# A stored list of 133 numbers that shifts the planned order of issue is replaced by a list of 201 others (clustered attention and a two-layer network, one core)

## The chip, the cores and the metric

The kernel runs on one core of one Trainium2 chip. The metric is device time in microseconds (us), from the first to the last instruction of one execution with what lies around it. Three runs of the kernel before are shown.

## The reference, cut to what matters

```python
# q, k, v: (4, 8, 768, 64) f32; centroids: (8, 16, 64); w_in (512, 2048); w_out (2048, 512)
q_assign = argmax(q_n . c_n)          # cluster of each query, k_assign the same for keys
mask   = q_assign[:, :, :, None] == k_assign[:, :, None, :]
scores = where(mask, q k^T / 8, -1e9)
attn   = softmax(scores)              # over 768 keys
x      = (attn v) as (3072, 512)      # heads side by side
h      = x @ w_in
g      = where(h >= 1, h, where(h <= -1, 0, (h + 1)^2 / 4))
out    = g @ w_out                    # (3072, 512) f32
```

All is float32 outside; inside, most products are made from pairs of float16 tiles (a high and a low half).

## The kernel before, in words

**Tiles.** The tokens are cut into 12 units `u` (4 batches of 3 chunks, 256 queries each). For each unit there are 4 pairs of heads. For one pair of heads the kernel makes 4 score tiles of 128 queries by 768 keys (`at_scores`, line 915): four products of 384 columns on TensorE into the PSUM tile `pair`, then one pass of VectorE that writes the tile to `sS` with its row minimum `sbi`. `at_soft` (line 946) exponentiates on ScalarE, makes the high half on ScalarE and the low half on GpSimd (`hl`), and sends `hl` through a transposing DMA to `pT`. For unit 0 (`whole`) the transposes are TensorE products instead. `at_av` (line 994) multiplies `pT` with the values into `banka`: 8 small and 36 larger products. Then follows the network: for each of 8 slabs `f`, `ffn1` (line 1149) does 24 products of 256 columns, VectorE and ScalarE apply the function, GpSimd makes the low half of `g`, and `ffn2` (line 1189) does 12 products of 512 columns.

**Preparation.** Before they are used, keys, queries and values are scaled and split (`k_split`, `q_split`, `v_split`), clusters assigned (`k_assign`, `q_assign`, `q_pairs`), and the 16 slabs of weights unpacked by integer passes on VectorE (`w_bits`, line 1081: tiles `w`, `word`, `wk`, `o`) and split on ScalarE and GpSimd (`w_split`, line 1138). The weights are prepared once, in the first fifth of the execution.

**The order of issue.** The functions don't issue anything: a `Recorder` (line 78) keeps each operation, or each group of products, as a node with an engine, a cost and the nodes it depends on. Each call of a function is an event (`ev`); sorted by the step at which it was entered there are 852 of them, and the set-up before them counts as one more, so 853. `issue` (line 328) makes the order: nine rounds of a forward and a backward pass of a list scheduler give each node a due time in ns, each number of the list `NUDGES` (line 45) shifts some due times, and a last forward pass with these due times as priorities fixes the order in which the instructions go to each engine's queue. Then the recorded calls are made in that order, all from line 342, so every row of the profile bears that line. Engines take their queues in order. All DMAs are issued from SP's queue, so their order is fixed by the same pass.

**What one number does** (`nudge`, line 314). It is hashed to a first event `lo`, a count of 1 to 128 events, a stride of 1, 2 or 5 and a size of 500 to 8000 ns; the due times of the nodes in these events move by a hashed share of plus or minus the size:

```python
lo, every, size = b % len(names), (1, 2, 5)[(a >> 8) % 3], float(500 << ((a >> 16) % 5))
...
    if lo <= i < lo + (1 << (a % 8)) and not (i - lo) % every:
        r = c if c >> 8 & 1 else mix(c + i * 7919)
        prio[x] += ((r & 0xFFFF) / 32768.0 - 1.0) * size
```

The forward pass (line 215) lets each engine take, among nodes whose inputs have come, the one with the smallest due time. Its model of the chip (`Machine`, line 345) knows a cost per instruction, a fixed lag per engine, the DMA queue, a slower TensorE after little work, and a turn that VectorE and GpSimd take with some of their passes.

Of the kernel before, what the change touches and what calls it, by code (L numbers as in the profile page):

```python
# [42 lines left out]
LOOK, MARGIN = 0.4, 4000  # L43
BASE = 9
NUDGES = (
# [17 lines left out]
)  # L63
TILED = 248

# [1283 lines left out]
```

## Time and profile before

| | us |
|---|---|
| runs of the kernel before | 855.63, 849.04, 852.69 (median 852.69) |
| span of the profiled execution | 851.1 |
| TensorE (PE) busy in it | 810.1 |
| VectorE (DVE), ScalarE (ACT), GpSimd (POOL) busy | 635.3, 656.1, 536.2 |

The page gives the span of the profiled execution, and no time of its own beside it. PE's busy time counts a product from its start to its modelled end; idle time of PE is the span less this. A releaser is what ended an idle time. Times inside a view are us from the start of the span.

### The profile page before, as it was taken

What the parts mean: (1) busy time and instruction counts of PE and PEld (TensorE: products, weight loads), DVE (VectorE), ACT (ScalarE), POOL (GpSimd) and SP (SyncE); (2) the same over time, 40 slices, a digit from 0 to 9 for tenths busy, and PEclk for the clock granted to TensorE, in tenths of its full rate; (3) what the DMA queues carried; (4) which work ended last, traced back from release to release, by engine and by line L of the source; (5) the groups of instructions that cost most, each with busy time, mean ns of one, the idle gap of its engine ahead of it and who ended that gap; (6) DMA issues with size and microseconds to landing.
All of it is one profiled execution on the core that took longest, in us unless ns stands there. A gap on an engine that the chain in (4) does not pass through costs nothing.

```text
span 851.1 us, 18767 instructions
## 1 busy us (share of the span) xinstructions
PE 810.1 (95%) x7052; PEld 558.9 (66%) x7052; DVE 635.3 (75%) x1400; ACT 656.1 (77%) x1166; POOL 536.2 (63%) x510
## 2 busy tenths in 40 slices
PE   3787998999999999999999999999999999999998
PEld 3455675666775676766776667667766667676664
DVE  6999999879886877678888766678888766544322
ACT  7778989899987788688778788788778688776232
POOL 1112799879986678667666778656677667666122
PEclk9999999999999999999999999999999999999999
DMA  9968898798999879898998988999999887665100
GB/s 311 269 138 246 225 204 213 157 172 194 186 172 159 186 128 205 171 185 169 201 187 165 168 160 177 197 170 199 204 155 161 150 162 126 119 123 111 20 25 25
DMA packets 404763, 142.50 MB, mean 167 GB/s; under 512 B 372800, under 2 KB 396352, under 8 KB 404672
## 3 DMA queue, kind: packets, MB, share of 16 engines
q1 hardware_dynamic: 404672, 141.30, 82.1%
q8 instruction: 55, 0.90, 0.4%
q14 instruction: 36, 0.29, 0.1%
HBM read 40.40 MB, written 6.29 MB: 55 GB/s over the span
## 4 chain that ended last, share of the span: by engine, by line
PE 77%; DVE 12%; DMA 4%; issue 3%; ACT 2%; POOL 1%; SPq 0%; DVEq 0%; POOLq 0%; ACTq 0%
PE pair L342 39%; PE banka L342 10%; PE banki L342 9%; PE bankj L342 9%; PE bankh L342 9%; DVE sS L342 3%; DVE w L342 2%; DMA pT<-hl 1%; DVE bankh L342 1%; DMA q<-qn 1%; DMA kv<-n 1%; ACT sS L342 1%; DVE mx L342 1%; DMA kv<-x 1%; POOL hl L342 1%
## 5 line engine op out<-in xcount | busy, mean ns | idle before, releaser
L342 POOL TENSOR_TENSOR hl<-sS,hl 128x768 f16<-128x768 f32 x176 | 301.2, 1716 | 120.7 <-ACT hl L342 105.5
L342 PE MATMUL pair<-w,g 128*128 128x512 f16 (+1 forms) x1120 | 276.7, 392 | 0.7 <-DVE g L342 0.7
L342 ACT ACTIVATE sS<-sS,sbi 128x768 f32<-128x768 f32 x192 | 179.2, 933 | 73.9 <-DVE sbi L342 70.5
L342 DVE CUSTOM_DVE_ANT_0 sS<-pair,zero,er 128x768 f32<-128x768 f32 x192 | 194.3, 1012 | 53.6 <-PE pair L342 32.9
L342 PEld LDWEIGHTS <-w 128*128 128x128 f16 x2112 | 204.9, 98 | 42.7 <-issue 4.5
L342 PEld LDWEIGHTS <-g 128*128 128x128 f16 x1056 | 101.1, 98 | 107.2 <-issue 2.0
L342 PE MATMUL pair<-kv,q 128*128 128x384 f16 x768 | 158.1, 329 | 11.1 <-ACT pT L342 5.0
L342 ACT CAST hl<-sS 128x768 f16<-128x768 f32 x176 | 144.4, 825 | 9.3 <-DMA pT<-hl 7.9
L342 POOL TENSOR_TENSOR g<-r,g 128x512 f16<-128x512 f32 x80 | 96.4, 1205 | 56.4 <-ACT g L342 50.6
L342 PEld LDWEIGHTS <-q 128*128 128x128 f16 x992 | 78.9, 98 | 66.6 <-issue 22.8
L342 PE MATMUL banka<-pT,kv 128*64 128x256 f16 (+1 forms) x1680 | 105.7, 279 | 0.3 <-DMA pT<-hl 0.3
L342 PEld LDWEIGHTS <-kv 128*64 128x64 f16 (+1 forms) x1824 | 92.3, 108 | 5.0 <-DMA kv<-x 1.7
L342 ACT ACTIVATE r<-r,f_ra,f_rs 128x512 f32<-128x512 f32 x80 | 64.8, 810 | 35.0 <-DVE r L342 34.3
L342 PE MATMUL bankj<-x,w 128*128 128x256 f16 (+1 forms) x424 | 59.1, 292 | 0.6 <-DVE g L342 0.4
L342 ACT CAST g<-r 128x512 f16<-128x512 f32 x80 | 48.8, 611 | 11.8 <-DVE r L342 5.9
L342 POOL TENSOR_TENSOR qn<-qn,phi 128x256 f16<-128x256 f16 x48 | 31.9, 684 | 30.3 <-DVE phi L342 19.9
L342 PE MATMUL bankh<-x,w 128*128 128x256 f16 (+1 forms) x376 | 46.7, 277 | 0.6 <-DVE zs L342 0.5
L342 PE MATMUL banki<-x,w 128*128 128x256 f16 (+1 forms) x288 | 40.3, 291 | 0.9 <-DVE r L342 0.9
L342 PE MATMUL banki<-wk,w 128*128 128x256 f16 x312 | 37.0, 273 | 0.0
L342 ACT ACTIVATION_READ_ACCUMULATOR sS<-sS,sbi 128x1 f32 x192 | 36.1, 188 | 0.0
L342 ACT ACTIVATE q<-q,phi 128x512 f16<-128x512 f16 x48 | 33.0, 711 | 2.8 <-DVE phi L342 0.8
L342 DVE TENSOR_SCALAR r<-banki,f_lo,f_hi 128x512 f32<-128x512 f32 x27 | 21.8, 806 | 16.0 <-PE banki L342 10.0
(262 smaller groups left out, 1099.8 us busy)
## 6 DMA issues: line engine op xcount, KB each, us to landing
w<-in_moe_w_out_dram SPq DMA_DIRECT2D x14, 512.0 KB, 4.8
q<-in_q_dram SPq DMA_DIRECT2D x12, 512.0 KB, 5.4
kv<-in_k_dram SPq DMA_DIRECT2D x16, 384.0 KB, 4.0
kv<-in_v_dram SPq DMA_DIRECT2D x16, 384.0 KB, 4.4
out_dram<-o SPq DMA_DIRECT2D x11, 512.0 KB, 3.6
w<-in_moe_w_in_dram SPq DMA_DIRECT2D x10, 512.0 KB, 6.1
word<-in_moe_w_in_dram SPq DMA_DIRECT2D x6, 512.0 KB, 4.3
o<-in_v_dram SPq DMA_DIRECT2D x8, 384.0 KB, 3.9
```

The costliest lines, as they stand in the source:

```text
L342: fn(*args, **kw)
```

## The change

The 133 numbers of `NUDGES` are replaced by 201 others, none of which was in the old list. The old numbers are close together (2100000010 to 2100031687), in ascending order; the new ones are spread over 32 bits and in no order. They are said to come from a new search with many more evaluated orders, and with replays in which results come late at random. Nothing else is edited: the same nodes, costs, buffers, and the same model.

```diff
 NUDGES = (
-    2100000010, 2100000020, 2100000029, 2100000041, 2100000053, 2100000117, 2100000135, 2100000137,
...
-    2100027979, 2100028867, 2100030528, 2100031297, 2100031687,
+    2274640804, 3868013745, 1465309218, 3554455116, 1849672550, 1493886748, 838542255, 1618903720, 2841474855,
...
+    3685093637, 53219364, 3824218690,
 )
```

Hashing the numbers as `nudge` does tells which events they touch: the old list touches 1,734 events in all (an event counted each time it is touched), 130 of them among the first 213 of the 853; the new one 2,378, and 840 of them among the first 213. Event 213 lies at step 41, in the third unit of the twelve.

## Rows read from the trace of the kernel before

**Rows 1.** The page: the span, and busy time of each engine with its share.

```profile
span 851.1 us, 18767 instructions
PE 810.1 (95%) x7052; PEld 558.9 (66%) x7052; DVE 635.3 (75%) x1400; ACT 656.1 (77%) x1166; POOL 536.2 (63%) x510
```

**Rows 2.** Busy time by stretch, six stretches that make up the span. Columns: stretch, length, then busy us (and instructions) of PE, PE's weight loads, DVE, ACT and POOL, the granted clock of PE as a share of full speed, the DMA engines' busy share, GB/s.

```profile
0.00:22.10 22.10, 8.91 (x123) 8.09 (x124) 13.98 (x46) 16.66 (x27) 3.17 (x28) 1.00 0.93 310
22.10:85.10 63.00, 46.39 (x443) 31.18 (x441) 60.14 (x151) 47.44 (x83) 11.08 (x18) 0.95 0.85 217
85.10:190.00 104.90, 99.22 (x693) 67.84 (x692) 95.17 (x171) 95.28 (x157) 85.82 (x55) 0.98 0.89 194
190.00:340.00 150.00, 149.12 (x1350) 102.50 (x1350) 123.55 (x282) 129.09 (x235) 120.04 (x109) 1.00 0.93 176
340.00:839.30 499.30, 498.73 (x4417) 345.93 (x4414) 339.94 (x750) 364.61 (x663) 313.79 (x300) 1.00 0.79 150
839.30:851.10 11.80, 7.78 (x37) 3.33 (x34) 2.53 (x4) 3.00 (x5) 2.31 (x2) 0.94 0.12 44
```

**Rows 3.** The same columns for the stretch between 20.5 and 163.8 alone.

```profile
20.50:163.80 143.30, 121.91 (x934) 82.91 (x932) 136.19 (x263) 119.67 (x197) 77.86 (x59) 0.96 0.88 211
```

**Rows 4.** What PE waited for between 22.1 and 85.1: us in total, times, longest.

```profile
PE pair L342 <- ACT sS L342: 5.5, 8, 0.9
PE pair L342 <- ACT pT L342: 5.0, 7, 1.4
PE pair L342 <- DMA kv<-n: 1.4, 1, 1.4
```

**Rows 5.** The same between 85.1 and 190, all rows.

```profile
PE pair L342 <- DVE sbi L342: 3.4, 1, 3.4
PE pair L342 <- ACT pT L342: 0.9, 1, 0.9
PE banki L342 <- DVE r L342: 0.9, 1, 0.9
PE pair L342 <- DVE g L342: 0.7, 1, 0.7
PE bankj L342 <- DVE g L342: 0.4, 1, 0.4
```

**Rows 6.** The three stretches in which PE's granted clock fell, with the columns of rows 2.

```profile
37.55:40.96 3.41, 3.41 (x22) 1.79 (x22) 3.10 (x10) 1.48 (x3) 1.30 (x4) 0.55 1.13 352
78.50:81.92 3.42, 3.42 (x25) 2.91 (x24) 3.42 (x6) 2.50 (x6) 0.00 (x0) 0.55 0.91 308
143.36:146.77 3.41, 2.96 (x13) 2.29 (x11) 2.84 (x6) 3.12 (x7) 3.41 (x4) 0.55 1.02 261
```

**Rows 7.** DVE's passes by form between 0 and 85: count, busy us, mean ns of one, and idle time before them.

```profile
L342 DVE CUSTOM_DVE_ANT_0 sS<-pair,zero,er 128x768 f32<-128x768 f32 x18 | 18.2, 1013 | 1.4 <-PE pair L342 1.3
L342 DVE SCALAR_TENSOR_TENSOR w<-w 128x1024 uint32<-128x1024 uint32 x6 | 7.5, 1253 | 0.0
L342 DVE SCALAR_TENSOR_TENSOR w<-w,o 128x1024 uint32<-128x1024 uint32 x4 | 4.9, 1226 | 0.0
L342 DVE SCALAR_TENSOR_TENSOR w<-w,wk 128x1024 uint32<-128x1024 uint32 x3 | 3.8, 1280 | 0.0
L342 DVE TENSOR_SCALAR o<-o 128x1024 uint32<-128x1024 uint32 x4 | 2.7, 686 | 0.0
L342 DVE TENSOR_SCALAR wk<-wk 128x1024 uint32<-128x1024 uint32 x4 | 2.7, 686 | 0.0
L342 DVE SCALAR_TENSOR_TENSOR hl<-kv,sv,hl 128x768 f16<-128x768 f32 x1 | 1.0, 1035 | 0.0
```

**Rows 8.** The same forms between 85 and 170.

```profile
L342 DVE CUSTOM_DVE_ANT_0 sS<-pair,zero,er 128x768 f32<-128x768 f32 x20 | 20.2, 1010 | 4.2 <-POOL hl L342 1.5 <-PE pair L342 1.4 <-issue 0.9
L342 DVE SCALAR_TENSOR_TENSOR w<-w 128x1024 uint32<-128x1024 uint32 x6 | 9.5, 1577 | 0.0
L342 DVE SCALAR_TENSOR_TENSOR w<-w,o 128x1024 uint32<-128x1024 uint32 x3 | 4.7, 1553 | 0.0
L342 DVE SCALAR_TENSOR_TENSOR hl<-kv,sv,hl 128x768 f16<-128x768 f32 x3 | 4.4, 1473 | 0.0
L342 DVE TENSOR_SCALAR wk<-wk 128x1024 uint32<-128x1024 uint32 x4 | 4.0, 998 | 0.0
L342 DVE SCALAR_TENSOR_TENSOR w<-w,wk 128x1024 uint32<-128x1024 uint32 x2 | 2.9, 1433 | 0.0
L342 DVE TENSOR_SCALAR o<-o 128x1024 uint32<-128x1024 uint32 x3 | 2.6, 873 | 0.0
```

**Rows 9.** Instructions in order of time around the longest wait of rows 5: start, length, engine, operation. The first two are DVE's, then two of POOL's, the next DVE's, the last PE's; the row at 72.80 is the same DVE pass at an earlier place.

```profile
137.85 1.74 DVE L342 SCALAR_TENSOR_TENSOR w<-word 128x1024 uint32<-128x1024 uint32 x1
139.51 1.87 DVE L342 TENSOR_TENSOR bankh<-zs,has 128x256 f32<-128x256 f32 x1
...
138.47 2.62 POOL L342 TENSOR_TENSOR hl<-sS,hl 128x768 f16<-128x768 f32 x1
141.06 2.38 POOL L342 TENSOR_TENSOR qn<-qn,phi 128x256 f16<-128x256 f16 x3
...
141.29 1.01 DVE L342 CUSTOM_DVE_ANT_0 sS<-pair,zero,er 128x768 f32<-128x768 f32 x1
...
142.36 0.81 PE L342 MATMUL pair<-kv,q 128*128 128x384 f16 x4 [3.40 <-DVE sbi L342]
...
72.80 0.45 DVE L342 TENSOR_TENSOR banki<-zs,has 128x256 f32<-128x256 f32 x1
```

**Rows 10.** PE's products of attention with the values (f16 tiles) over the whole span, by form, and the one place where they waited.

```profile
L342 PE MATMUL banka<-pT,kv 128*64 128x256 f16 x1584 | 94.2, 273 | 0.3 <-DMA pT<-hl 0.3
...
471.87 2.15 PE L342 MATMUL banka<-pT,kv 128*64 128x256 f16 x35 [0.26 <-DMA pT<-hl]
```

36 rows, old and new, of the table NUDGES are left out of this document.

## The prediction

> **What bounds the kernel now.** I read the page first: PE is busy for 810.1 of 851.1 us, the other engines for 63 to 77% [rows 1]. So 41.0 us of PE's idle time is all that an order of issue can win, apart from what it does to the length of single instructions. Next come the stretches, to see where the 41 us lie [rows 2]. The reader is to see three regimes. From 0 to 22.1 PE is idle for 13.2 us, while the first tiles come in. From 22.1 to 85.1 it is idle for 16.6 and from 85.1 to 190 for 5.7. From 190 to 839.3, three quarters of the span, it is idle for 0.88 + 0.57 = 1.45 us, so no order can win there. The last 11.8 us hold 4.0 us of idle time, the evacuation and the last store.
>
> In the second regime the bound is another engine. Between 20.5 and 163.8 DVE is busy for 136.19 of 143.30 us (95%), PE for 121.91 [rows 3]. PE's waits there name ACT (`sS`, `pT`), many of them short [rows 4]; further on DVE itself is named for most of the idle time [rows 5]. But ACT is only at 119.67 of 143.30 in that stretch, so it is a link in the chain product, DVE pass, ACT pass, transpose, and DVE is what that chain queues behind. Reading further down DVE's own rows: the score pass keeps its length between the two halves of this regime (1013 and 1010 ns), while the passes that unpack weights and split values grow [rows 7, 8].
>
> So the end of the kernel is set thus: DVE paces the start until about 164 us, and from there on PE works through what is left without a gap. Each microsecond by which DVE's early work ends sooner moves the end by at most a microsecond; each microsecond of a new gap after 190 moves it by a whole one.
>
> **The change, part by part.** No operation is removed, added or resized: every count and every tile stays, the DMAs too, and by itself that costs nothing. What moves is the order within the five queues, SP's with all the DMAs included. Where it moves can be told from the numbers: 840 of the 2,378 touches of the new list fall on the first 213 of 853 events, against 130 of 1,734, and these events, up to the third unit, are where rows 2 have nearly all the idle time. The old list left the order of this part nearly as the due times had it; the new one reorders it throughout. That the start changes is therefore certain; the sign is not. I cost it by what is there to be won, term by term.
>
> (a) DVE's idle time while it paces: 143.30 - 136.19 = 7.1 us [rows 3]. Bounds: 7.1 won, or as much lost again. I take half, 3.6, because most of the score passes' idle time in the later part has releasers (`hl` of POOL, `pair` of PE, issue) [rows 8] whose order is free.
>
> (b) DVE passes that grow between the two parts [rows 7, 8]: `w<-w` (1577 - 1253) x 6 = 1.94 us; `w<-w,o` (1553 - 1226) x 3 = 0.98; `w<-w,wk` (1433 - 1280) x 2 = 0.31; `wk` (998 - 686) x 4 = 1.25; `o` (873 - 686) x 3 = 0.56; `hl<-kv` (1473 - 1035) x 3 = 1.31; and the pass on `has` took 1.87 where 0.45 is seen at 72.80 [rows 9], 1.42. Together 7.8 us. POOL is busy for 11.08 of 63.00 us in the earlier part and 85.82 of 104.90 in the later [rows 2]. Rows 9 show one meeting: a POOL pass of 2.62 us runs from 138.47 to 141.09 and DVE's pass on `has` ends at 141.38, only then does the score pass run, and PE stands for 3.40 us. Bounds: 7.8 won, or (POOL moved earlier beside the 21 weight passes of rows 7, at the mean growth of the weight passes above, 5.04 / 18 = 0.28 us each) 5.9 lost. With POOL at 82% of this stretch most meetings must stay whatever the order; I take a quarter won, 2.0.
>
> The Trainium skill ("SBUF — State Buffer", section "SBUF: two separate sides") says that a VectorE pass with two SBUF inputs, or in a two-port mode, and a GpSimd pass share one pair of ports as an exclusive lock, and that the one which comes second is blocked in full. Rows 9 agree, 1.87 us for a pass of 0.45 that ends 0.29 us after POOL's. By the page, an order that never lets DVE come second would win all of (b), and one that always does would lose more than I take.
>
> (c) PE's slower stretches. Three times the granted clock reads 0.55, so mostly at the 1.2 GHz level, each time after a stretch in which PE had waited much; the lost work is 0.45 x (3.41 + 3.42 + 2.96) = 4.4 us [rows 6]. The first two lie where DVE paces anyway, and PE's lost work is covered by waits that would else be longer. The third follows the gap of 3.40 us. It is worth 1.3 if it goes, and another such stretch the same if one comes. I take half, 0.7.
>
> (d) The first 22.1 us hold 13.2 us of idle time; PE is waiting for loads and the first chain of scaling and splitting, with little else to issue. Between a gain of 3.6 (the longest wait behind the first product is of that order: DVE's idle time there is 22.10 - 13.98 = 8.1) and a loss of as much, I take nothing.
>
> (e) After 190: nothing to win (1.45), and as much to lose as the order is careless with. I take nothing here; it is the third case below.
>
> Sum: 3.6 + 2.0 + 0.7 = 6.3 us, so 851.1 - 6.3 = 844.8 for an execution like the profiled one. The span shown is 1.6 below the median of the three runs, 852.69; against the median the forecast is 846.4, and I put 846.
>
> **The rivals.** *First, the larger gain.* The whole of (a), (b) without remainder of its larger parts and the third slow stretch: 7.1 x 0.5 + 7.8 + 1.3 = 12.7, so 852.7 - 12.7 = 840.0; with all of (a) 836.5. For it: the largest single gap of the later part (3.40 us) comes straight from one meeting of DVE and POOL and a queue behind it, which one exchange of two passes undoes, and PE has 22.3 us idle between 22.1 and 190 to fill. The rule on the shared ports is the same case, (b) in full: 852.7 - 7.8 = 844.9 by it alone. Against it: POOL's 85.82 us of work in 104.90 have to lie beside something.
>
> *Second, slower, by late transposes.* The attention products for 44 pairs of heads (1584 / 36) each wait for a transposing DMA that follows ACT and POOL; now only one of them waits, for 0.26 us [rows 10]. PE's queue is in order, so a group put closer behind its transposes stops everything. If every group waited as that one did, 44 x 0.26 = 11.4 us and 864.1. It decides from 8.5 / 44 = 0.19 us each. For it: the DMA engines are at 0.93 between 190 and 340 [rows 2], so a transpose that is moved meets other traffic. Against it: the old order keeps 43 of 44 free of waits, and the same due times still stand under the new list.
>
> *Third, no net effect.* What is won in one place before 164 comes back as another wait of the same regime, since DVE's 136.19 us are work that must be done: 852.7, from 848 to 858. This takes in that the list does not do what it is said to: whether an order bears late results can't be seen in one that was not run, and slack bought for late results may cost a later start.
>
> **How the numbers follow.** A measurement of this kernel can tell about 1% from no change, 8.5 us. Chances: the forecast (gain of about 2 to 9 us) 0.39; the larger gain 0.35; slower by late transposes 0.12; no net effect 0.14. A tail of 0.02 of the forecast and all of the larger gain lie below 844.2: faster 0.37. Of the last case 0.01 lies above 861.2: slower 0.13. Within 1%: 0.50. The range of 8 in 10 reaches from the larger gain with (a) in full, 837, to the upper end of the case without net effect, 858; the cases of a gain alone would give 837 to 851.
>
> **What would show it.** Right for (a) and (b): DVE's busy share between 20.5 and PE's last gap up from 95%, the `w` passes of the later part back near 1.25 us, PE's full stretch beginning before 164. Right for (c): the granted clock below 1.00 in two stretches or fewer after 22 us. The larger gain: PE's idle time between 22.1 and 190 below 12 us. The slower case: waits of PE on `pT<-hl` after 190 in many rows, and PE's idle time there well above 1.45. Wrong altogether: a changed idle time in the first 22 us, or PE busy time other than 810 by more than the slow stretches explain, since I hold both fixed.

## The result, and the profile after

The changed kernel takes 860.14 us (median of 5 runs, 858.79 to 861.35) against 851.87 for the kernel before in the same comparison: a ratio of 1.0091, with an interval of 1.0069 to 1.0113. It is slower by 0.9%, where 846 us were forecast with a range up to 858.

The page of the changed kernel, its first lines, to be held against [rows 1]:

```profile
span 859.6 us, 18776 instructions
PE 810.5 (94%) x7052; PEld 558.3 (65%) x7052; DVE 644.6 (75%) x1400; ACT 658.6 (77%) x1166; POOL 533.2 (62%) x510
```

PE does the same work in the same time (810.5 us against 810.1), so the 8.5 us of span are idle time of PE. The number that moved most beside the span is DVE's: 644.6 us for the same 1,400 instructions that took 635.3, 9.3 more.

Busy time by stretch, changed kernel, with the columns of [rows 2]; the last row is the stretch of [rows 3]:

```profile
0.00:22.10 22.10, 8.96 (x123) 8.03 (x124) 12.93 (x45) 16.09 (x26) 3.17 (x28) 1.00 0.89 303
22.10:85.10 63.00, 47.95 (x464) 31.56 (x463) 61.09 (x155) 48.89 (x85) 11.51 (x19) 0.95 0.91 224
85.10:190.00 104.90, 96.90 (x654) 66.05 (x651) 96.49 (x169) 93.04 (x155) 81.78 (x54) 0.98 0.83 186
190.00:340.00 150.00, 143.75 (x1324) 99.82 (x1323) 124.34 (x275) 124.64 (x226) 113.66 (x104) 1.00 0.88 169
340.00:840.00 500.00, 497.38 (x4403) 343.65 (x4401) 344.10 (x752) 370.73 (x670) 319.60 (x305) 1.00 0.81 152
840.00:859.60 19.60, 15.51 (x96) 9.16 (x94) 5.65 (x8) 5.24 (x8) 3.46 (x3) 1.00 0.07 28
20.50:163.80 143.30, 122.42 (x931) 82.71 (x929) 135.70 (x264) 119.79 (x198) 74.28 (x58) 0.96 0.89 213
```

PE's idle time, length less busy time, before and after: 13.2 and 13.1 us up to 22.1; 16.6 and 15.1 up to 85.1, a gain of 1.6; 5.7 and 8.0 up to 190; 0.9 and 6.3 up to 340; then 0.6 and 2.6 up to the last stretch, and 4.0 and 4.1 in it. Up to 190 the two orders are nearly level (0.7 us lost in sum). The loss comes after that, most of it (5.4 us) between 190 and 340, where the old order left PE hardly a gap.

What PE waited for there, first between 190 and 340, then from 340 on, all rows (us in total, times, longest):

```profile
PE bankj L348 <- DVE r L348: 1.9, 2, 0.9
PE pair L348 <- DVE sbi L348: 1.8, 3, 1.0
PE bankh L348 <- DMA kv<-n: 1.4, 1, 1.4
PE banki L348 <- DVE n L348: 1.2, 1, 1.2
...
PE pair L348 <- DVE sbi L348: 1.2, 2, 1.0
PE bankh L348 <- DVE r L348: 1.0, 1, 1.0
PE banki L348 <- DMA kv<-n: 0.4, 1, 0.4
```

Of 8.9 us, 7.1 end with DVE, and in nearly all cases with a pass that is itself no longer than usual. To see what made it late one goes back along DVE's row, as far as DVE had no idle time. One place of several, the wait at 438.68 (DVE, POOL, PE; start, length):

```profile
434.31 0.36 DVE L348 TENSOR_SCALAR n<-bankj 128x192 f16<-128x192 f32 x1
434.70 1.61 DVE L348 SCALAR_TENSOR_TENSOR bankj<-ik,iq 128x1 f32<-128x1 f32 x1
...
437.61 1.01 DVE L348 CUSTOM_DVE_ANT_0 sS<-pair,zero,er 128x768 f32<-128x768 f32 x1
...
434.64 1.65 POOL L348 TENSOR_TENSOR hl<-sS,hl 128x768 f16<-128x768 f32 x1
...
438.68 0.81 PE L348 MATMUL pair<-kv,q 128*128 128x384 f16 x4 [0.98 <-DVE sbi L348]
```

A DVE pass of one column per partition takes 1.61 us. A pass of POOL started 0.06 us ahead of it and ended at 436.29; DVE's ended at 436.31. Five passes further on comes the score pass, and PE stands for 0.98 us.

The kernel's own planner gives each operation a planned start, so the trace can be laid beside the plan, pass by pass. In the plan this DVE pass starts 0.16 us ahead of the POOL pass; on the chip it came behind. I call a DVE pass **overtaken** when the plan starts it before a POOL pass and the trace shows it held by that pass for over 0.15 us. In the old order's trace 8 DVE passes are overtaken, for 8.8 us in all, 1.0 us of it between 190 and 340. In the new order's trace there are 24, for 26.5 us, 10.7 of it between 190 and 340. In the plan these 24 passes are ahead by 0.07 to 1.02 us. Of PE's nine waits for DVE after 190, eight (all but one of 0.24 us) lead back along DVE's row to an overtaken pass. The plan itself ends at 844.8 us for the old list and at 841.8 for the new: by the planner the new list is 3 us better.

An overtaken pass need not cost PE anything. In the old order the same one-column pass is overtaken too, and PE does not wait there:

```profile
429.13 0.95 DVE L342 SCALAR_TENSOR_TENSOR bankj<-ik,iq 128x1 f32<-128x1 f32 x1
```

In the new plan the products at 438.68 start less than 0.01 us after their score pass is due, so the lost turn reaches PE. Not every place is that tight, and the new plan is not tighter on the whole: after 190, 42 groups of products are planned to start within 0.5 us of the DVE result that they wait for, against 43 in the old plan.

### The profile page after: what moved, and what is told of

Read it like the earlier page. It is cut to its first block, busy times and chain, and to the rows that moved or that the text cites. A ratio compares the mean times of both kernels' runs of the same rounds, so it can differ in the third digit from the quotient of the medians.

```text
span 859.6 us, 18776 instructions
## 1 busy us (share of the span) xinstructions
PE 810.5 (94%) x7052; PEld 558.3 (65%) x7052; DVE 644.6 (75%) x1400; ACT 658.6 (77%) x1166; POOL 533.2 (62%) x510
## 4 chain that ended last, share of the span: by engine, by line
PE 64%; DVE 18%; DMA 7%; ACT 5%; issue 4%; POOL 1%; SPq 0%; DVEq 0%; ACTq 0%; POOLq 0%
PE pair L348 32%; PE banka L348 9%; PE banki L348 9%; PE bankj L348 8%; PE bankh L348 7%; DVE sS L348 4%; DMA pT<-hl 2%; DVE w L348 2%; DVE r L348 2%; DMA kv<-n 1%; ACT sS L348 1%; DVE bankh L348 1%; DVE qn L348 1%; DVE banki L348 1%; ACT hl L348 1%
## 5 line engine op out<-in xcount | busy, mean ns | idle before, releaser
L348 PEld LDWEIGHTS <-w 128*128 128x128 f16 x2112 | 205.0, 98 | 45.6 <-issue 6.2
L348 POOL TENSOR_TENSOR g<-r,g 128x512 f16<-128x512 f32 x80 | 94.3, 1179 | 54.3 <-ACT g L348 54.1
```

The source lines that it names most:

```text
L348: fn(*args, **kw)
```

## The experiments

Two theories. **Turns**: the new order loses because POOL passes reach the ports that, by this theory, they share with DVE ahead of DVE passes which the plan had put first, sometimes by less than 0.1 us, and DVE then stands for most of a POOL pass. **Slack**: the new order has too little room for late results of any kind, and the ports are only where one happens to see it.

**POOL's passes kept, their reading taken away.** POOL's subtracting passes become a pass of 8 columns, which keeps the wait for ACT, and two fills. The order of issue is kept, since it is made from the recorded operations before this. The low halves are left out of the result.

```diff
+if x.eng == "gpsimd" and kw.get("op") == ALU.subtract and self.free(o) > 16:
+    fn(out=o[:, :8], in0=kw["in0"][:, :8], in1=kw["in1"][:, :8], op=ALU.subtract)
+    for _ in range(2):
+        self.nc.gpsimd.memset(o[:, 8:], 0.0)
+    continue
```

> The new order as it is, but GpSimd's five kinds of subtracting passes (low halves of hl, g, w, x) do 8 columns only and then fill the rest with zeros in two write-only passes, so that they take about as long and still wait for ScalarE, but hardly read beside VectorE; the low halves are left out of the result. Theory 'turns': the new order loses because GpSimd passes get ahead of VectorE passes that the plan had put first, and VectorE stands for the length of a GpSimd pass; then without that the loss goes: 840 to 848 us, no more than 2 us above old_apart, PE's idle time between 190 and 340 from 6.25 to below 2.5 us. Rival 'slack': the new order leaves too little room for any late result, whatever makes it late; then it stays 6 to 9 us above old_apart, with 5 us or more of PE idle time between 190 and 340.

> The old order with the same replacement of GpSimd's passes. Theory 'turns': the old order had 8 VectorE passes overtaken against 24 of the new one, so it gains less: 843 to 849 us. Rival 'slack': 850 to 853, nothing to gain since its results came in time.

Measured: 844.63 us with the new order (ratio to the kernel before 0.9915, interval 0.9896 to 0.9934), 846.85 with the old (0.9940, 0.9924 to 0.9956). POOL's groups by form and PE's waits after 85.1 in the new order's run, then its page and a stretch:

```profile
span 842.5 us, 19343 instructions
PE 806.2 (96%) x7052; PEld 558.1 (66%) x7052; DVE 599.0 (71%) x1400; ACT 658.2 (78%) x1166; POOL 519.1 (62%) x1158
...
L352 POOL MEMSET hl<- 128x760 f16 x352 | 257.7, 732 | 10.1
L350 POOL TENSOR_TENSOR hl<-sS,hl 128x8 f16<-128x8 f32 x176 | 41.7, 237 | 119.3 <-ACT hl L354 116.4 <-DVE sbi L354 2.2
...
PE bankh L354 <- DMA kv<-n: 1.2, 1, 1.2
PE pair L354 <- DVE sbi L354: 1.2, 1, 1.2
PE banki L354 <- DVE w_am L354: 0.3, 1, 0.3
...
190.00:340.00 150.00, 148.80 (x1367) 103.56 (x1366) 110.38 (x278) 128.88 (x237) 115.06 (x256) 1.00 0.94 177
```

A pass on `hl` takes 0.24 + 2 x 0.73 = 1.70 us, as the subtraction did (1.705 in the changed kernel), so POOL is nearly as busy as before (519.1 us, it was 533.2). DVE is not: 599.0 us where it was 644.6. So 45.6 us of DVE's busy time came from standing beside POOL passes that read. PE's idle time between 190 and 340 falls from 6.25 to 1.20 us. And the new order is now the better one by 2.2 us, nearly the 3 us by which its plan is. That is what turns expected (idle time below 2.5 us) and not what slack expected (6 to 9 us above the old order, 5 us idle). But the run also frees DVE of more than the 26.5 us of overtaken passes, which gives room to late results of any kind, so it does not decide alone. The runs with added waits, which keep all the work, must do that.

**The same in the middle alone.** The replacement only where `180e3 < x.start < 330e3` in the plan.

> The new order with the replacement of new_apart in its middle alone: the 74 subtracting GpSimd passes that the plan starts between 180 and 330 us (on the chip some 190 to 345), and so with the low halves left out there. Theory 'turns': the gap that opened in this stretch closes, 5 to 7 us off 860, 853 to 855.5 us, with PE's idle time between 190 and 340 from 6.25 to below 2. If the loss of this stretch is carried in from the start instead: 857 to 860.

Measured: 854.70 us (850.68 to 857.96, a wider spread than the others), ratio 1.0029 (1.0007 to 1.0051): 5.4 us below 860.14. PE's idle time between 190 and 340 is 1.22 us. So the gap of this stretch arises in it and is not carried in. The 5.4 us of time are less sure than the gap: nothing was edited before 180, and still the profiled execution has two stretches at a granted clock of 0.50 there (from 33.17 and 70.72) where the changed kernel has three, and PE is busy for 806.5 us in place of 810.5. So part of a difference between two executions can be the clock.

**The planned turn, enforced, all work kept.** A POOL pass that the plan starts within 1.5 us after the end of the last DVE pass that shares its ports waits for that pass. Such near pairs number 195 in the new order and 186 in the old.

```diff
+if x.turn and x.eng == "vector":
+    last = x, i
+if x.turn and x.eng == "gpsimd" and last and x.start < last[0].busy + 1500:
+    self.tc.add_manual_dep(i.ins, last[1].ins.name, ...)
```

> The new order, all work in it, with one more wait: a GpSimd pass that the plan starts within 1.5 us after the end of the last VectorE pass that shares its ports waits for that pass (195 of 469). Theory 'turns': 844 to 853 us, the VectorE passes that were overtaken back at their planned length, PE's idle time between 190 and 340 below 3 us. Rival 'slack': 858 to 864, since GpSimd's results only come later.

> The old order with the same wait (186 of 469). Theory 'turns': 845 to 851 us, a gain of about half of what the new order gains. Rival 'slack': 852 to 856.

Measured: 854.58 us for the new order (1.0027, 1.0014 to 1.0040), 854.43 for the old (1.0022, 1.0010 to 1.0035). The new order gets 5.6 us back, 1.6 short of what turns expected, with PE's idle time between 190 and 340 at 2.29 us, as it expected; the old one loses 1.9, which was expected by slack and not by turns. In both traces no DVE pass is overtaken any more. But DVE passes that the plan has behind POOL's are now held for 45.5 us in the old order, where it was 33.2: a POOL pass that waits where nothing was to be gained runs later, and can meet the next DVE pass. So I read it that the wait has a price where it was not needed; no run takes these waits away one by one.

**The wait only where the trace shows an overtaken pass.** 24 pairs for the new order, 8 for the old, by number of the recorded operation:

```diff
+PINS = {458: (417,), 476: (525,), 558: (565,), ...}
...
+    for y in PINS.get(x.i, ()):
+        self.tc.add_manual_dep(i.ins, made[y].ins.name, ...)
```

> The new order, with the added wait at 24 places alone: those where the trace of the changed kernel shows a VectorE pass that the plan had put ahead of a GpSimd pass and that stood behind it (26.5 us of VectorE's time in all). Theory 'turns': most of the loss comes back, 849 to 855 us, better than with all 195 waits (854.6), some of it kept because other passes meet instead. Rival 'slack': 858 to 861.

> The old order with the wait at its 8 such places (8.8 us of VectorE's time, 5.6 of them before 190 us). Theory 'turns': 847 to 852 us, below the kernel before if the five early places weigh as they look. Rival 'slack': 852 to 855.

Measured: 849.74 us for the new order with 24 waits (0.9962, 0.9947 to 0.9977), 850.44 for the old with 8 (0.9984, 0.9970 to 0.9998). The 24 waits give back 10.4 us, more than the whole loss; slack expected 858 to 861. The clock is no rival for this: in executions with a mean granted clock of 0.993 and 0.994 the changed kernel took 858.79 and 861.35 us, and at 0.994 the one with 24 waits took 849.62 to 850.38. In the profiled executions the spans differ by 13.8 us, of which 3.3 are PE's busy time (two stretches at 0.50, from 64.19 and 71.01, where the changed kernel has three) and the rest idle time. The place of above in this run:

```profile
423.44 0.36 DVE L350 TENSOR_SCALAR n<-bankj 128x192 f16<-128x192 f32 x1
423.83 0.17 DVE L350 SCALAR_TENSOR_TENSOR bankj<-ik,iq 128x1 f32<-128x1 f32 x1
...
424.23 1.64 POOL L350 TENSOR_TENSOR hl<-sS,hl 128x768 f16<-128x768 f32 x1 [0.42 <-DVE bankj L350]
...
426.66 0.81 PE L350 MATMUL pair<-kv,q 128*128 128x384 f16 x4
```

POOL stands for 0.42 us, the one-column pass takes 0.17, and PE's products follow without a wait: 0.42 us of POOL, for which PE does not wait here, in place of 1.44 us of DVE and 0.98 of PE.

**Four more waits**, where the trace of that run still shows an overtaken pass.

> new_pin_few with the wait at four more places, those where its own trace still shows a VectorE pass overtaken (3.5 us in all). Theory 'turns': little is left to win, 848 to 850.5 us. Rival, that the 24 waits gained by chance of a new order of events and not by these turns: it can go anywhere between 846 and 856.

Measured: 847.72 us (0.9948, 0.9933 to 0.9963), faster than both kernels: 0.5% below the kernel before, and 0.3 us under what turns expected. The time alone also lies in the rival's range (846 to 856, a chance of a new order of events). The trace speaks for turns: it shows no overtaken pass, and after 190 no wait of PE for DVE. The page's span and busy line, two stretches, and all of PE's waits from 190 on:

```profile
span 845.2 us, 18780 instructions
PE 806.8 (95%) x7052; PEld 556.9 (66%) x7052; DVE 624.3 (74%) x1400; ACT 658.9 (78%) x1166; POOL 529.7 (63%) x510
...
85.10:190.00 104.90, 100.43 (x708) 69.01 (x705) 96.17 (x176) 98.52 (x163) 85.95 (x58) 1.00 0.91 195
190.00:340.00 150.00, 148.81 (x1371) 103.14 (x1370) 119.61 (x282) 129.01 (x235) 115.46 (x109) 1.00 0.93 175
...
PE bankh L350 <- DMA kv<-n: 1.1, 1, 1.1
```

**Other orders.** No list at all, the new list without its last 20 numbers, and two lists that I searched with replays of my own.

> No numbers at all: the order that the nine rounds of due times give. The plan ends at 852.0 us, against 844.8 with the old list and 841.8 with the new. If the chip is behind the plan by a fixed amount (7 us as with the old list): 859. If the loss of the new list is what a list fitted to the plan pays, an order that was not fitted is behind by less: 855 to 859. If every order has its 18 us: 870.

> The new list without its last 20 numbers; the plan ends at 841.7 us, as with all 201. Theory 'turns': how many passes are overtaken is chance for orders of equal plan, so it may differ from the new list's 860.1 by several us either way, 852 to 862; behind the old list's order, whose plan has more to spare. Rival 'slack': within 2 us of 860.

> 57 other numbers, searched from no list in the same planner by replays in which the order of each queue is kept, each result comes up to 0.1 us early or late (VectorE's 0.03 later on average) and whoever of VectorE and GpSimd is ready first takes its turn; the plan alone ends at 844.7 us, its replays at 846.8, those of the old order at 852.9 and of the new one at 854.8. If such replays tell an order that holds on the chip: 845 to 850 us, below the kernel before, with fewer than 10 overtaken VectorE passes. If they don't (as the list of this change, said to be searched with late results): 852 to 860.

> The old list with 44 more numbers from the same search, plan 845.0 us, replays 847.3. 846 to 851 us if the replays tell it; 852 to 858 if not.

| order | plan, us | chip, us | chip less plan | overtaken DVE passes, their us |
|---|---|---|---|---|
| no list | 852.0 | 855.99 | 4.0 | 4, 5.7 |
| old list | 844.8 | 851.87 | 7.0 | 8, 8.8 |
| old list and 44 more (jit_old) | 845.0 | 850.44 | 5.5 | 6, 6.6 |
| 57 others (jit_none) | 844.7 | 851.83 | 7.2 | 13, 15.3 |
| new list less 20 | 841.7 | 857.49 | 15.8 | 15, 17.7 |
| new list | 841.8 | 860.14 | 18.4 | 24, 26.5 |
| new list, 24 waits | 841.8 | 849.74 | 8.0 | 4, 3.6 |
| new list, 28 waits | 841.8 | 847.72 | 6.0 | 0, 0 |
| new list, 195 waits | 841.8 | 854.58 | 12.8 | 0, 0 |
| old list, 8 waits | 844.8 | 850.44 | 5.6 | 3, 3.2 |
| old list, 186 waits | 844.8 | 854.43 | 9.6 | 0, 0 |

The new list is slower than no list, which ends where an order that was not fitted was expected (855.99, of 855 to 859). The plans of the orders with waits are those without them. In the rows without waits the chip is mostly further behind the plan where more passes are overtaken; jit_none does not fit, with 13 passes and 7.2 us, so the number of lost turns does not tell the loss by itself. The two orders with a wait at every near pair don't fit either: none is overtaken, and they are 12.8 and 9.6 us behind. With no overtaken pass left, 6.0 us remain at the least. Two orders of equal plan (the list with and without its last 20 numbers) differ by 2.7 us, where slack expected at most 2. My own replays did not tell what holds: they promised some 6 us over the old order, and jit_none gave nothing (1.0005, 0.9993 to 1.0016), with 13 overtaken passes where fewer than 10 were expected; jit_old gave 0.15% (0.9985, 0.9971 to 0.9998), within what was expected of it. Choosing an order by such replays was no remedy here, a wait at the pass in question was.

## Why the prediction was wrong

- **What bounds the kernel** held: DVE paces the start (135.70 of 143.30 us, last row of the stretches above), PE the rest, and PE's busy time and the first 22 us stayed.
- **(a)** was not won: DVE's idle time in that stretch is 143.30 - 135.70 = 7.6 us, where it was 7.1. PE's idle time between 22.1 and 85.1 fell by 1.6 us, the one gain of the new order that the trace shows, and the next stretch gave 2.3 back.
- **(b)** had the right mechanism, and won on the passes that it priced, but not in the stretch. Those seven kinds of pass took 52.8 us up to 190 before and 49.5 after, 3.3 less where I took 2.0. Others grew instead, which I had not priced: `w<-n,o`, one pass of 512 columns, from 0.73 to 2.40 us, and `w<-word`, below. So turns changed hands, and DVE's early work did not end sooner. I also looked for the meeting of DVE and POOL only where DVE paces, up to 170. The [rows 9] meeting was a planned one; what matters is which of the two comes first, and the new order lost that 24 times, 17 of them after 190. I measured it mostly by wide passes; of those 17, 14 have 256 columns or fewer, such as the one-column pass above. Two of the priced kinds and an unpriced one between 0 and 190, before and after:

```profile
L342 DVE SCALAR_TENSOR_TENSOR w<-w 128x1024 uint32<-128x1024 uint32 x12 | 17.0, 1415 | 0.0
L342 DVE SCALAR_TENSOR_TENSOR hl<-kv,sv,hl 128x768 f16<-128x768 f32 x4 | 5.5, 1364 | 0.0
L342 DVE SCALAR_TENSOR_TENSOR w<-word 128x1024 uint32<-128x1024 uint32 x3 | 4.6, 1529 | 0.0
...
L348 DVE SCALAR_TENSOR_TENSOR w<-w 128x1024 uint32<-128x1024 uint32 x12 | 15.4, 1291 | 0.0
L348 DVE SCALAR_TENSOR_TENSOR hl<-kv,sv,hl 128x768 f16<-128x768 f32 x4 | 4.0, 1010 | 0.0
L348 DVE SCALAR_TENSOR_TENSOR w<-word 128x1024 uint32<-128x1024 uint32 x3 | 5.4, 1804 | 0.1
```

- **(c)** was not won either: the trace has three stretches of 3.41 us at a granted clock of 0.50 again (1.2 GHz, from 64.53, 71.36 and 119.15). That [rows 6] read 0.55 before is a matter of the windows, which lie 0.3 us late: from 37.23, 78.19 and 143.04 they read 0.50 too.
- **(e)** is the step that failed: "After 190: nothing to win (1.45), and as much to lose as the order is careless with. I take nothing here". The loss was put at nothing without a reason; the third case, to which it points, deals with gains before 164. PE's idle time there went from 1.45 us to 8.87, of which 7.1 end with DVE, nearly all behind passes that POOL had overtaken, and the 24 added waits, 17 of them after 190, gave 10.4 us back: with them PE is idle for 1.2 us from 190 to 830. That PE is full did not mean that DVE has room: PE takes its products in order, and those of the place shown were planned to start less than 0.01 us after their DVE pass was due.
- **The rivals.** The slower one had the right sign and the right place (PE's queue, after 190), but named transposes; they are 1.8 of 8.9 us, none of it on `pT`. The rule of the Trainium skill ("SBUF — State Buffer", section "SBUF: two separate sides") stood beside (b) with the sentence that an order in which DVE always comes second would lose more than I took. A loss of that kind is what happened, at 24 passes, and among the rivals I had the rule only as a case of gain. The case without net effect ended at 858, 2 us short of the measured time.
- **The base** was right by luck. I took 1.6 us between the span and the median as a difference of executions. The runs now show times and spans together, such as 861.35 and 859.6: 1.7 to 2.1 us lie around every span.

What stays open: which of the planner's costs lets POOL and DVE drift apart by 0.1 to 2.2 us; why jit_none loses so little with 13 overtaken passes; what makes the 6 us that remain with none; whether waits at 24 other near pairs would give anything; and how the late replays behind the new list were made. The kernel holds only their result, so whether they let a turn change hands is not known.

## What to carry to other kernels

An order found by search on a model can lean on turns that the chip does not keep. It was not the number of close turns that set the two orders apart (195 near pairs against 186) but how many were lost, 24 against 8, so the trace has to tell which. Pin those with a wait where the engine that is made to wait has time, rather than search longer, and pin only those: the same wait at all 195 near pairs gave 5.6 us back, at the 24 that had been overtaken 10.4. When an engine gets busier with the same instructions, ask first what holds them: busy time in a profile can be waiting.

## What the runs showed of the hardware

- A VectorE pass of one column took 1.61 us behind a GpSimd pass that had started 0.06 us earlier, and 0.17 with the turn kept. The 1.44 us lost go with the length of the other's pass (1.65), not with one's own.
- GpSimd's passes that only write did not hold VectorE's passes with two SBUF inputs: `qn<-q,sq,qn` took 649 ns on average in the changed kernel, up to 1867, and 478 with the fills, at most 486. The Trainium skill ("SBUF — State Buffer", section "Who interferes with whom") says so of a VectorE pass with two SBUF inputs; these runs agree.
- A fill can still hold a VectorE pass with one input: the pass on `zs` below took 0.81 us (its shortest is 0.28) and ended 0.15 us after the fills beside it, which ran up to 649.06.

```profile
L348 DVE SCALAR_TENSOR_TENSOR qn<-q,sq,qn 128x256 f16<-128x256 f32 x48 | 29.8, 649 | 3.8 <-ACT qn L348 3.6
...
L354 DVE SCALAR_TENSOR_TENSOR qn<-q,sq,qn 128x256 f16<-128x256 f32 x48 | 21.5, 478 | 3.5 <-ACT qn L354 3.4
...
647.54 1.52 POOL L352 MEMSET hl<- 128x760 f16 x2
648.40 0.81 DVE L354 TENSOR_SCALAR qn<-zs 128x256 f16<-128x256 f32 x1
```
